# Window attention: tiles of 128 queries of one head become tiles of 64 queries of two heads, and a list scheduler orders the stage

## The chip, the cores and the metric

The kernel runs on one core of a Trainium2 chip. A core has five engines that work side by side, each through its own queue in order: TensorE (PE, matrix products and transpositions; its weight loads are PEld), VectorE (DVE), ScalarE (ACT), GpSimd (POOL) and SyncE (SP), which here issues most of the DMA transfers. PSUM is eight banks into which TensorE writes; SBUF holds the rest; both have 128 partitions. The metric is the device time of one execution in microseconds (us).

## The reference, cut to what matters

Three steps follow each other: attention with a causal window of 128 positions, a layer with a rational nonlinearity, a layer with an ELU.

```python
B, H, S, D = 4, 8, 576, 64
scores = q @ k.T / sqrt(D)                      # per batch entry and head
bias = -slopes[h] * abs(rel)                    # rel = query position - key position
mask = (rel >= 0) & (rel < 128)
attn = softmax(where(mask, scores + bias, -1e9))
x = (attn @ v), heads side by side              # (2304, 512)
h = x @ w_in;  x = (P(h) / Q(h)) @ w_out        # 512 -> 2048 -> 512, P and Q polynomials
h = x @ w_in2; out = elu(h) @ w_out2            # 512 -> 2048 -> 512
```

## The kernel before

All numbers are fp32 or fp32 split into a high and a low part for the large products. The attention runs in 16 units (`units`): a unit `u` is one batch entry and one pair of heads (`e` = 0, 1). Its steps have short names that the change keeps in spirit:

- `q_T`/`k_T` steps (`qT`, `kT`, `zT`) transpose q and k on TensorE; `qC`, `kC`, `zC` copy them out of PSUM to `qkT`. The last 64 positions (576 = 4 x 128 + 64) are a tail of their own, in the bank `ty`.
- `S0` to `S3` are the scores of 128 queries of each head against up to 256 keys (two products, one a head, on the two row halves of the array, each with a bank of its own); `S4` is the tail: 64 queries of both heads, stacked on the partitions, in one bank.
- `D0` to `D8` (`shifted`, VectorE) add the bias of the window and find the row's maximum in one instruction; `E0` to `E8` (`exp`, ScalarE) exponentiate and sum; `R0`, `R1` (`inverse`, VectorE) invert the sums; `N0` to `N8` (`normalise`, GpSimd) multiply.
- `T..` transpose the probabilities on TensorE, `C..` copy them out (ScalarE), `V0`, `V1`, `Y` multiply by v, `XC` and `XY` copy the unit's result into `xT`.

Beside it the stage converts the first layer's weights for the later products, key by key: `s` (ScalarE), `a`, `b`, `h`, `l` (`conv_scale`, `conv_shift`, `conv_or`, `conv_hi`, `conv_lo`), two keys a unit from the fourth unit on (`PLAN`), four more near the end (`CONV_AFTER`, where `conv_hi` is ScalarE's). Loads of q, k, v (`load`) and weights (`load_w`) are issued on SP.

What sets the order is the table `STEPS`: one period is run through step by step, and each step is for unit `t + late`, so that the units overlap. Towards the end the first four chunks of the next stage's first product (`early`, `AHEAD`) and the first two rational nonlinearities (`FIRST`) are put between. `experts` follows with the two layers.

## Time and profile before

| what | value |
|---|---|
| time, median of 3 runs | 932.98 us (931.71 to 934.49) |
| time of the profiled execution | 933.09 us |
| its span, first to last instruction | 931.4 us |
| busy in the span: TensorE, VectorE, ScalarE, GpSimd | 98%, 85%, 80%, 20% |
| granted TensorE clock | 0.998 of full |

The span is less than the execution's time by what lies ahead of the first and behind the last instruction. Busy shares are means over stages: the attention stage, about the first 150 us, is not limited as the rest is, where TensorE multiplies without a gap.

### The profile page before, as it was taken

To read this page: it belongs to the slowest core of one execution; us is meant where nothing else is said; L and a number is where in the kernel's file an instruction comes from. 1 tells how busy PE (TensorE), PEld (TensorE's weight loads), DVE (VectorE), ACT (ScalarE), POOL (GpSimd) and SP (SyncE) were. 2 spreads that over 40 slices of the span, in tenths; PEclk is the share of its full clock that TensorE was granted. 3 is DMA by queue.
4 is the path that set the end of the run, shared out by engine and by line. 5 is a ranking of instruction groups with operands and counts; after the bars stand their busy time and mean duration, and the time that the engine had idled before them with its cause. 6 is when DMAs were issued, how large, how long until landed. Compare 5 with 4: busy or idle time off the path is not lost.

```text
span 931.4 us, 16710 instructions
## 1 busy us (share of the span) xinstructions
PE 913.8 (98%) x5494; PEld 838.8 (90%) x5494; DVE 792.0 (85%) x1863; ACT 741.9 (80%) x1623; POOL 185.2 (20%) x260
## 2 busy tenths in 40 slices
PE   8999999999999999999999989999999999999998
PEld 5777778999999999999999988898989898888887
DVE  7899998998998998988989999998968688677653
ACT  6999999889898898889888987666876567767553
POOL 5566661122222222222222210000000000000000
PEclk9999999999999999999999999999999999999999
DMA  9899951012222212222200133445243323442201
GB/s 195 217 242 230 236 154 67 1 35 68 86 68 79 89 56 92 85 63 86 86 30 29 38 110 113 158 157 171 91 162 110 115 81 100 147 147 80 80 0 68
DMA packets 112423, 98.35 MB, mean 106 GB/s; under 512 B 62800, under 2 KB 86096, under 8 KB 112336
## 3 DMA queue, kind: packets, MB, share of 16 engines
q1 hardware_dynamic: 109936, 96.70, 35.2%
q10 hardware_dynamic: 2400, 0.59, 0.4%
q8 instruction: 43, 0.70, 0.3%
q14 instruction: 44, 0.36, 0.1%
HBM read 79.96 MB, written 17.30 MB: 104 GB/s over the span
## 4 chain that ended last, share of the span: by engine, by line
PE 79%; DVE 14%; ACT 3%; DMA 2%; issue 1%; DVEq 0%; ACTq 0%; SPq 0%
PE acc L923 21%; PE m L907 18%; PE acc L699 18%; PE h L251 18%; DVE pr_wi L494 2%; DVE pr_wo L494 1%; DVE cvt L146 1%; PE s_ps L468 1%; DVE qkT L437 1%; DVE ghi L292 1%; PE x L561 1%; DVE ee L313 1%; DMA q_wo<-in_q_dram 1%; PE ps_pT L542 1%; DVE w_wi L160 1%
## 5 line engine op out<-in xcount | busy, mean ns | idle before, releaser
L251 PE MATMUL h<-xs,w_wi 128*128 128x384 f32 x1152 | 216.9, 335 | 0.0
L251 PEld LDWEIGHTS h<-xs,w_wi 128*128 128x128 f32 x1152 | 200.7, 188 | 1.2 <-DVE xs L227 0.6
L699 PE MATMUL acc<-ghi,w_wo 128*128 128x384 f32 x768 | 194.8, 334 | 0.0
L310 POOL TENSOR_TENSOR glo<-ee,rr 128x384 fp32r<-128x384 f32 x92 | 93.7, 1018 | 312.4 <-DVE ee L309 109.3
L699 PEld LDWEIGHTS acc<-ghi,w_wo 128*128 128x128 f32 x768 | 138.6, 188 | 0.0
L699 PE MATMUL acc<-glo,w_wo 128*128 128x384 f32 x384 | 128.4, 334 | 0.5 <-DVE glo L310 0.5
L923 PE MATMUL acc<-op_wo,ghi 128*128 128x512 f32 x288 | 90.0, 393 | 0.0
L907 PE MATMUL m<-xo_wo,op_wi 128*128 128x384 f32 x336 | 77.0, 337 | 2.3 <-DVE ee L963 2.3
L907 PE MATMUL m<-xo_wi,op_wi 128*128 128x384 f32 x336 | 78.0, 340 | 0.0
L969 ACT ACTIVATE oo<-qq 128x384 f32<-128x384 f32 x24 | 12.6, 526 | 77.0 <-DVE qq L963 77.0
L699 PEld LDWEIGHTS acc<-glo,w_wo 128*128 128x128 f32 x384 | 72.1, 188 | 0.8 <-DVE glo L310 0.8
L298 ACT ACTIVATE rr<-qq,c_q 128x384 f32<-128x384 f32 x96 | 59.2, 617 | 16.5 <-DVE qq L295 15.7
L281 ACT ACTIVATE oo<-h,a_sb 128x384 f32<-128x384 f32 x96 | 68.0, 708 | 3.3 <-DVE h L312 3.2
L284 ACT ACTIVATE ee<-h,a_sb 128x384 f32<-128x384 f32 x96 | 67.7, 705 | 0.0
L907 PEld LDWEIGHTS m<-xo_wo,op_wi 128*128 128x128 f32 x336 | 61.3, 189 | 6.4 <-ACT oo L973 2.5
L295 DVE SCALAR_TENSOR_TENSOR qq<-h,b_abs,qa 128x384 f32<-128x384 f32 x92 | 56.1, 610 | 12.4 <-ACT qa L280 11.3
L292 DVE TENSOR_TENSOR ghi<-ee,rr 128x384 fp32r<-128x384 f32 x96 | 53.5, 558 | 12.2 <-ACT h L279 0.5
L313 DVE TENSOR_TENSOR ee<-ee,h 128x384 f32<-128x384 f32 x96 | 53.3, 555 | 10.4 <-DVE h L312 0.5
L923 PEld LDWEIGHTS acc<-op_wo,ghi 128*128 128x128 f32 x288 | 53.8, 189 | 9.0
L907 PEld LDWEIGHTS m<-xo_wi,op_wi 128*128 128x128 f32 x336 | 61.1, 189 | 0.0
L279 ACT ACTIVATE h<-h 128x384 f32<-128x384 f32 x96 | 46.3, 483 | 14.8 <-PE h L251 14.2
L963 DVE TENSOR_TENSOR ee<-ee,m 128x384 f32<-128x384 f32 x96 | 52.8, 551 | 5.8 <-PE m L907 5.5
(192 smaller groups left out, 2068.4 us busy)
## 6 DMA issues: line engine op xcount, KB each, us to landing
pair<-joined_wo SPq DMA_DIRECT2D x43, 256.0 KB, 2.6
raw_wo<-in_moe_w_out_dram SPq DMA_DIRECT2D x20, 512.0 KB, 4.7
raw_wi<-in_moe_w_in_dram SPq DMA_DIRECT2D x16, 512.0 KB, 4.3
half<-in_moe_w_in_dram SPq DMA_DIRECT2D x32, 256.0 KB, 2.7
two_wo<-joined_wi SPq DMA_DIRECT2D x32, 256.0 KB, 2.8
s<-sums SPq DMA_DIRECT2D x32, 256.0 KB, 2.9
half<-in_moe_w_out_dram SPq DMA_DIRECT2D x22, 256.0 KB, 2.8
v<-in_v_dram SPq DMA_DIRECT2D x32, 128.0 KB, 3.3
```

Source lines behind the costliest of these rows:

```text
L251: nc.tensor.matmul(h, lhsT=WT["wi", f][:, SEL[wp], kk * P:(kk + 1) * P], rhs=x[xp][kk], start=(kk == 0 and n == 0), stop=(kk == KD - 1 and ...
L281: nc.scalar.activation(out=oo, in_=h2, func=AF.Identity, scale=a_sb[:, 3:4], bias=a_sb[:, 1:2])
L284: nc.scalar.activation(out=ee, in_=h2, func=AF.Identity, scale=a_sb[:, 2:3], bias=a_sb[:, 0:1])
L292: nc.vector.tensor_tensor(out=hi, in0=ee0, in1=rr0, op=ALU.mult)
L295: nc.vector.scalar_tensor_tensor(out=qq, in0=h2, scalar=b_abs[:, 1:2], in1=qa, op0=ALU.mult, op1=ALU.add)
L298: nc.scalar.activation(out=rr, in_=qq, func=AF.Ln, bias=c_q)
L310: (nc.gpsimd if c > 4 else nc.vector).tensor_tensor(out=low, in0=ee0, in1=rr0, op=ALU.mult)
L313: nc.vector.tensor_tensor(out=ee, in0=ee, in1=h, op=ALU.add)
L699: nc.tensor.matmul(acc_t[d], lhsT=WT["wo", f][:, SEL[wp], d * P:(d + 1) * P], rhs=gt[SEL[xp]], start=(f == 0 and n == 0), stop=(f == KF - ...
L907: nc.tensor.matmul(out, lhsT=w[:, SEL[wp], c0:c0 + P], rhs=XO[q // NP2, nm, k][:, SEL[xp]], start=(k == 0 and n == 0), stop=(k == 1 and n ...
L923: nc.tensor.matmul(acc_t[T, t], lhsT=gt[SEL[xp]][:, t * P:(t + 1) * P], rhs=w[:, SEL[wp]], start=(first and n == 0), stop=(last and n == 2),)
L963: nc.vector.tensor_tensor(out=t, in0=R[q, x], in1=M[q, m], op=ALU.add)
```

## The change

Attention is cut anew. A tile is now 64 queries (`Q`) of both heads stacked on the 128 partitions, nine tiles (`t` = 0 to 8) a unit, against the 64, 128 or 192 keys (`W`) that the window reaches; tiles alternate which head is on top. So the scores of a tile are two products on 64 x 64 corners of the array, and each of the steps `D`, `E`, `N` works on up to 192 columns where it had up to 256. Transposed probabilities are `T0` to `T3` (four or three blocks); the product with v is in 64-column pieces, even tiles in the bank `evens`, odd ones in `odds`, which also takes the last transpositions of q and k (`zC` copies these out). `XE` and `XO` copy the result out; `XY` is gone. The biases are rebuilt for this layout, all four pairs' early.

The table `STEPS` goes. `attention_steps` lists every step of the stage, loads, conversions (28 keys, `conv_hi` always on VectorE), the four chunks of the first product (`g`) and two nonlinearities (`r`) among them, each with its engine, a cost and what it needs; `in_time` then walks through them as a list scheduler with ranks (`rank`: 7600 a unit plus an offset of the step, `OFF`) and hands them out in order of the times it finds. Three banks of the next stage's first product rotate in another order.

```diff
-STEPS = (
-    ("T00", -1), ("a0", 1), ("l1", -1), ("C01", -1), ("S0", 1), ("S1", 1), ("C00", -1),
...
-    ("XC", -1), ("T01", 0),
-)
...
-PLAN = (0, 0, 0) + (2,) * 12 + (0,) * 4
-CONV_AFTER = ((15, "E8"), (15, "R1"), (14, "V1"), (15, "T01"), (15, "T11"), (15, "V1"))
-AHEAD = {
...
+UNITS = 16
+EARLY = 24
+LAG = {"PE": 250, "DVE": 150, "ACT": 190, "POOL": 180, "SP": 2300}
+UT = 7600
+MODE = {"qT": 0, "kT": 0, "T": 0, "S": 1, "V": 2}
+STAY = 800
...
+OFF = {
+    "ldq": -37303, "ldk": -40037, "ldv": -7307, "qT": 49228, "qC": -19956, "kT": -37687, "kC":
...
+def attention_steps():
+    todo = {}
+
+    def step(key, engine, cost, *needs):
+        todo[key] = (engine, cost, needs)
...
+    for u in range(UNITS):
+        p = u // 4
+        for n, nm in enumerate("qk"):
+            step(("ld", nm, u), "SP", 1550, (nm + "T", u - 2))
+        step(("ld", "v", u), "SP", 1550, ("V", u - 2, 1))
+        step(("qT", u), "PE", 590, ("ld", "q", u), ("ident",), ("consts",), ("kC", u - 1), ("zC", u - 1))
+        step(("kT", u), "PE", 590, ("ld", "k", u), ("ident",), ("consts",), *([("qC", u)] if u else []))
+        gone = [("S", u - 2, h) for h in range(2)]
+        step(("qC", u), "ACT", 477, ("qT", u), *gone)
+        step(("kC", u), "DVE", 603, ("kT", u), *gone)
+        step(("zC", u), "DVE", 200, ("kT", u), ("qT", u), *gone)
+        for h in range(2):
+            n = 2 * u + h
+            gone = []
+            for a in (2 * n - 3, 2 * n - 2):
+                v, g = divmod(a // 2, 2)
+                ts = [(0, 2, 4), (6, 8), (1, 3), (5, 7)][2 * (a % 2) + g]
+                gone += [("D", v, t) for t in ts]
+            step(("S", u, h), "PE", 750 - 110 * h, ("qC", u), ("kC", u), ("zC", u),
+                 ("S", u - 1 + h, 1 - h), *gone)
+        for t in range(9):
+            m = max(t - 1, 0) // 2
+            c = cols(t)
+            step(("D", u, t), "DVE", {64: 140, 128: 207, 192: 277}[c], ("S", u, int(t > 4)), ("bias", p),
+                 ("T", u - 2, m))
+            step(("E", u, t), "ACT", {64: 331, 128: 385, 192: 440}[c], ("D", u, t))
+            step(("N", u, t), "POOL", {64: 330, 128: 400, 192: 480}[c], ("R", u, int(t > 4)), ("E", u, t))
+        step(("R", u, 0), "DVE", 320, *[("E", u, t) for t in range(5)])
+        step(("R", u, 1), "DVE", 320, *[("E", u, t) for t in range(5, 9)])
+        for m in range(4):
+            v, w = divmod(4 * u + m - 2, 4)
+            step(("T", u, m), "PE", 440 if m == 0 else 330, *[("N", u, t) for t in tiles(m)], ("C", v, w),
+                 ("T", u - (m == 0), (m - 1) % 4))
+            step(("C", u, m), "ACT", 477 if m == 0 else 370, ("T", u, m), ("V", u - 1, m // 2))
+        for h in range(2):
+            step(("V", u, h), "PE", 1000, ("C", u, 2 * h), ("C", u, 2 * h + 1), ("ld", "v", u), ("XE", u - 1),
+                 ("XO", u - 1), *([("V", u, 0)] if h else []))
+        step(("XE", u), "ACT", 317, ("V", u, 0), ("V", u, 1))
+        step(("XO", u), "ACT", 264, ("V", u, 0), ("V", u, 1))
...
+        step(("ldw", n), "SP", 1550, *gone, ("ldw", n - 1))
+        if n >= EARLY + 4:
+            continue
+        step(("cs", n), "ACT", 588, ("ldw", n), ("cl", n - 3), ("cs", n - 1))
+        step(("ca", n), "DVE", 337, ("ldw", n))
+        step(("cb", n), "DVE", 577, ("cs", n), ("ca", n))
+        step(("ch", n), "DVE", 310, ("cb", n))
+        step(("cl", n), "DVE", 603, ("ch", n))
...
+    while len(order) < len(todo):
+        best = None
+        for engine, cand in ready.items():
+            if cand:
+                at = max(min(cand.values()), free[engine])
+                if best is None or at < best[0]:
+                    best = at, engine
+        at, engine = best
+        ends = MODE.get(last)
+        key = min(
+            (k for k, t in ready[engine].items() if t <= at + 40),
+            key=lambda k: ranks[k] + (engine == "PE" and MODE.get(k[0], ends) != ends and STAY),
+        )
...
+        if engine == "PE":
+            cost += 100 * (MODE.get(key[0], ends) != ends)
+            last = key[0]
+        free[engine] = at + cost
+        done[key] = at + cost + LAG[engine]
+        order.append((at, len(order), key))
...
-    def early():
-
-        for c in range(4):
-            yield from gemm1(c, c, x1[0], 4 + c)
...
-            def scores_tail(u):
-                qk = qkT_t[u]
-                s_t[u, 0] = sp = s_bank([P, P + TL])
-                for e in range(2):
-                    r0 = e * D
-                    nc.tensor.matmul(
-                        sp[e * TL:(e + 1) * TL, :],
-                        lhsT=qk[r0:r0 + D, 0, NF * P:S],
-                        rhs=qk[r0:r0 + D, 1, (NF - 1) * P:S],
-                        start=True, stop=True,
-                    )
-
-            def scores(i):
...
-                    for e in range(2):
-                        if i % 2 == 0:
-                            t = s_bank([P, 2, 2 * P])
-                            s_t[u, 1 + 2 * i + e] = t[:, 0]
-                            s_t[u, 3 + 2 * i + e] = t[:, 1]
-                        r0 = e * D
-                        nc.tensor.matmul(
-                            s_t[u, 1 + 2 * i + e][:, c0:2 * P],
-                            lhsT=qk[r0:r0 + D, 0, i * P:(i + 1) * P],
-                            rhs=qk[r0:r0 + D, 1, k0:k0 + 2 * P - c0],
-                            start=True, stop=True,
+                    r = raw_t["qk"[n], u]
...
+            def scores(u, h):
+
+                in_even, in_odd = [bank(next(s_banks), [P, 4 * P], "s_ps") for _ in range(2)]
+                qk = qkT[u % 2]
+                for t in ((0, 2, 1, 4, 3), (6, 5, 8, 7))[h]:
+                    w = min((t + 1) * Q, W)
+                    n = 2 if t == 0 else (t - 1) // 2 % 2
+                    s_t[u, t] = (in_odd if t % 2 else in_even)[:, n * W:n * W + w]
+                    for e in range(2):
+                        at = (e + t) % 2 * Q
+                        r = slice(e * D, (e + 1) * D)
+                        nc.tensor.matmul(
+                            s_t[u, t][at:at + Q], lhsT=qk[r, 0, t * Q:(t + 1) * Q],
+                            rhs=qk[r, 1, (t + 1) * Q - w:(t + 1) * Q], start=True, stop=True,
+                        )
...
+            def shifted(u, t):
+                sp = s_t.pop((u, t))
+                nc.vector.tensor_tensor_reduce(
+                    out=probs(u, t), in0=sp, in1=bias[units[u][1]][t % 2][:, W - sp.shape[1]:W],
+                    scale=-SC, scalar=BIG, op0=ALU.add, op1=ALU.min, accum_out=stat(u, 0, t, t + 1),
+                )
...
+            def attn_v(u, h):
+
+
+                vr = raw_t["v", u]
+                if h == 0:
+                    x_t[u] = bank(3, [P, NF + 1, Q], "evens")
+                todo = []
+                for m in (2 * h, 2 * h + 1):
+                    pT = pT_t[u, m]
+                    for e in range(2):
+                        todo.append((0, 0, e, m + 1, vr[:, m, e], pT[:, 2 + e]))
+                        todo.append((0, 1, e, m, vr[:, m, e], pT[:, 1 - e]))
+                        todo.append((1, 0, e, m + 1, vr[0:Q, m + 1, e], pT[0:Q, 4 + e]))
...
+                    nc.tensor.matmul(
+                        (x_t[u], odds)[to][e * D:(e + 1) * D, n], lhsT=lhsT, rhs=rhs,
+                        start=(to, e) not in begun, stop=(to, e) not in left,
                     )
...
+            def x_copy(n):
                 def run(u):
                     b, p = units[u]
-                    copy(eng, xT[:, p, b * S + NF * P:(b + 1) * S], ty[:, 2, :])
+                    x = xT[:, p, b * S:(b + 1) * S].rearrange("r (t c) -> r t c", c=Q)
...
-                for step, late in STEPS:
-                    run(step, t + late)
-                    if t < NU - 1 or not 0 <= t + late < NU:
...
-                    if (t + late, step) in CONV_AFTER:
-                        conv_step(to_conv, to_conv[0] not in LATE[4:])
-                    if (t + late, step) == FIRST["r0"]:
-                        rational(0)
...
+            for _, _, (name, *args) in in_time(attention_steps()):
+                if name != "ld" or args[0] == "v" or args[1] > 1:
+                    RUN[name](*args)
```

Three places of the order. The first is TensorE's queue in the middle of the stage; `s_ps` are scores, `ps_pT` transposed probabilities, `ps_qk` transposed q or k, `x`, `ty`, `evens`, `odds` products with v. Before:

```order
L542 MATMUL ps_pT<-ident,pr_wi_104 128x128 x3
L542 MATMUL ps_pT<-ident,rr_99 128x128
L542 MATMUL ps_pT<-ident,pr_wi_104 128x128 x4
L468 MATMUL s_ps<-qkT_101 128x128 x2
L468 MATMUL s_ps<-qkT_101 128x256 x2
L542 MATMUL ps_pT<-ident,pr_wo_105 128x128 x4
L412 MATMUL ps_qk<-ident,k_wo_1239 128x128 x4
L542 MATMUL ps_pT<-ident,pr_wo_105 128x128 x3
L542 MATMUL ps_pT<-ident,rr_99 128x128
L450 MATMUL s_ps<-qkT_101 64x192 x2
L468 MATMUL s_ps<-qkT_101 128x256 x4
```

After, a stretch of the same length in the stage:

```order
L581 MATMUL ps_qk<-ident,q_wo_89 128x128 x4
L581 MATMUL odds<-ident,q_wo_89 128x128
L675 MATMUL odds<-pT,v_93 64x64 x2
L675 MATMUL evens<-pT,v_93 64x64 x2
L675 MATMUL odds<-pT,v_93 64x64 x2
L675 MATMUL evens<-pT,v_93 64x64 x4
L675 MATMUL odds<-pT,v_93 64x64 x2
L675 MATMUL evens<-pT,v_93 64x64 x4
L645 MATMUL ps_pT<-ident,pr_wo_104 128x128 x3
L608 MATMUL s_ps<-qkT_99 64x192 x8
L645 MATMUL ps_pT<-ident,pr_wo_104 128x128 x3
```

Scores of 128 queries against 256 keys have become eight products of 64 x 192 in a row, and the product with v is 16 products of 64 columns at a time where it was 14 of 128 and 4 of 64 in three groups.

The second place is the copy of the last q and k columns of unit 15 from `odds`. On TensorE, after the transpositions of k into `odds`, the order now is:

```order
L581 MATMUL ps_qk<-ident,k_wo_91 128x128 x4
L581 MATMUL odds<-ident,k_wo_91 128x128
L645 MATMUL ps_pT<-ident,pr_wi_101 128x128 x3
L675 MATMUL odds<-pT,v_93 64x64 x2
L675 MATMUL evens<-pT,v_93 64x64 x2
L675 MATMUL odds<-pT,v_93 64x64 x2
L675 MATMUL evens<-pT,v_93 64x64 x2
L675 MATMUL odds<-pT,v_93 64x64 x2
L675 MATMUL evens<-pT,v_93 64x64 x2
L675 MATMUL odds<-pT,v_93 64x64 x2
L675 MATMUL evens<-pT,v_93 64x64 x2
```

and on VectorE the copy and its neighbours:

```order
L311 TENSOR_TENSOR w_wo_2153<-cvt_2123,w_wo_2153 128x512
L559 COPY qkT_99<-ps_qk 128x512
L629 TENSOR_SCALAR qq_100<-qq_100 128x5
L630 RECIPROCAL qq_100<-qq_100 128x5
L287 TENSOR_SCALAR raw_wi_2121<-raw_wi_2121 128x512
L559 COPY qkT_99<-odds 128x2x64
L615 ISA pr_wi_101,qq_100<-s_ps,rr_97 128x128
```

The copy from `odds` stands in program order behind the product with v of unit 11 that also writes that bank; before, it read the bank `ty`, with the tails.

The third place is VectorE's queue at the end of the stage, up to the first low part `glo` that the next stage's second product takes. Before:

```order
L160 TENSOR_TENSOR w_wi_2374<-cvt_2311,w_wi_2374 128x512
L295 SCALAR_TENSOR_TENSOR qq_2385<-h_2383,b_abs,qq_2385 128x384
L312 TENSOR_TENSOR h<-oo,h 128x384
L313 TENSOR_TENSOR ee_2384<-ee_2384,h 128x384
L160 TENSOR_TENSOR w_wo_2412<-cvt_2350,w_wo_2412 128x512
L437 COPY xT<-ty 128x64
L292 TENSOR_TENSOR ghi_2458<-ee_2328,rr_2331 128x384
L304 SCALAR_TENSOR_TENSOR qq_2329<-qq_2329,ghi_2458 128x384
L309 TENSOR_TENSOR ee_2328<-ee_2328,qq_2329 128x384
L310 TENSOR_TENSOR glo_2459<-ee_2328,rr_2331 128x384
```

After:

```order
L428 TENSOR_TENSOR h<-oo,h 128x384
L429 TENSOR_TENSOR ee_2606<-ee_2606,h 128x384
L305 CAST w_wi_2668<-cvt_2639 128x512
L287 TENSOR_SCALAR raw_wo_2614<-raw_wo_2614 128x512
L311 TENSOR_TENSOR w_wi_2668<-cvt_2639,w_wi_2668 128x512
L297 SCALAR_TENSOR_TENSOR cvt_2673<-cvt_2673,raw_wo_2614 128x512
L305 CAST w_wo_2697<-cvt_2673 128x512
L311 TENSOR_TENSOR w_wo_2697<-cvt_2673,w_wo_2697 128x512
L458 TENSOR_TENSOR ghi_2715<-ee_2520,rr_2523 128x384
L470 SCALAR_TENSOR_TENSOR qq_2521<-qq_2521,ghi_2715 128x384
L475 TENSOR_TENSOR ee_2520<-ee_2520,qq_2521 128x384
L476 TENSOR_TENSOR glo_2716<-ee_2520,rr_2523 128x384
```

The last conversions (L305 casts the high part, L311 subtracts it) and the second nonlinearity stand there as before; the casts of the high part are new in VectorE's queue, and the copies of the result from `ty` are gone.

## Rows read from the trace of the kernel before

**Rows 1.** The page of the profile: its first line.

```profile
span 931.4 us, 16710 instructions
```

**Rows 2.** Busy time by stretch, with its sum (stretch, length, engine busy and count).

```profile
core 0: us, PE busy (x) PEld busy (x) DVE busy (x) ACT busy (x) POOL busy (x), PEclk, DMA share, GB/s
0.00:9.20 9.20, 7.23 (x28) 3.43 (x28) 2.85 (x7) 2.48 (x3) 5.63 (x24) 1.00 1.01 171
...
60.00:120.00 60.00, 58.33 (x584) 43.21 (x584) 59.52 (x237) 59.30 (x187) 39.97 (x66) 1.00 0.94 226
...
sum 155.00, PE 143.86 PEld 107.74 DVE 138.71 ACT 143.34 POOL 91.51; mean PE 23.98 PEld 17.96 DVE 23.12 ACT 23.89 POOL 15.25
```

**Rows 3.** Timeline of TensorE (start, length, line, tiles, count): scores of two units.

```profile
60.58 0.93 PE L468 MATMUL s_ps<-qkT 64*128 64x128 f32 x8
...
77.55 0.71 PE L468 MATMUL s_ps<-qkT 64*128 64x128 f32 x6
```

**Rows 4.** Timeline of TensorE at the handover.

```profile
155.19 0.44 PE L699 MATMUL acc<-glo,w_wo 128*128 128x384 f32 x1 [0.51 <-DVE glo L310]
...
157.05 2.24 PE L251 MATMUL h<-xs,w_wi 128*128 128x384 f32 x12
```

**Rows 5.** Timeline of ScalarE: copies, exponentials, rounding of x.

```profile
76.83 0.58 ACT L435 ACTIVATE xT<-x 128x512 f32<-128x512 f32 x1
77.31 1.06 ACT L435 ACTIVATE pT<-ps_pT 128x512 f32<-128x512 f32 x2
...
81.80 0.51 ACT L509 ACTIVATE pr_wo<-pr_wo,qq 128x256 f32<-128x256 f32 x1
...
83.36 0.46 ACT L509 ACTIVATE rr<-rr,qq 128x192 f32<-128x192 f32 x1
...
134.37 1.75 ACT L226 ACTIVATE xs<-xT 128x384 fp32r<-128x384 f32 x4
```

**Rows 6.** Timeline of VectorE: end copy, shift-and-reduce, cast.

```profile
77.76 0.22 DVE L437 COPY xT<-ty 128x64 f32<-128x64 f32 x1
...
80.57 0.28 DVE L494 CUSTOM_DVE_ANT_0 pr_wo<-s_ps,oo 128x128 f32<-128x128 f32 x1
...
81.99 0.35 DVE L494 CUSTOM_DVE_ANT_0 rr<-s_ps,bias_t 128x192 f32<-128x192 f32 x1
...
82.87 0.41 DVE L494 CUSTOM_DVE_ANT_0 pr_wi<-s_ps,h 128x256 f32<-128x256 f32 x1
...
126.61 0.39 DVE L154 CAST w_wo<-cvt 128x512 fp32r<-128x512 f32 x1
```

**Rows 7.** Timeline of VectorE before its first shift-and-reduce.

```profile
4.37 0.34 DVE L389 SCALAR_TENSOR_TENSOR bias_t<-relmask_wi 64x192 f32<-64x192 f32 x1
...
9.21 0.29 DVE L494 CUSTOM_DVE_ANT_0 pr_wi<-s_ps,bias_wo 128x128 f32<-128x128 f32 x1 [1.38 <-PE s_ps L468]
```

**Rows 8.** Timeline of TensorE, unit 13 and its neighbours.

```profile
124.51 1.75 PE L561 MATMUL x<-pT,v 128*64 128x128 f32 x28
126.09 0.40 PE L572 MATMUL ty<-pT,v 128*64 128x64 f32 x8
...
127.44 0.93 PE L468 MATMUL s_ps<-qkT 64*128 64x128 f32 x8
128.30 0.98 PE L542 MATMUL ps_pT<-ident,pr_wo 128*128 128x128 f32 x7
```

**Rows 9.** Groups of TensorE by shape, 60 to 120 us: count | busy us, mean ns | idle.

```profile
L542 PE MATMUL ps_pT<-ident,pr_wi 128*128 128x128 f32 x54 | 8.5, 280 | 0.0
...
L450 PE MATMUL s_ps<-qkT 64*64 64x192 f32 x28 | 3.8, 348 | 0.0
```

**Rows 10.** Chain that ended last (start, length, what).

```profile
43.35 6.34 DMA q_wo<-in_q_dram
```

**Rows 11.** DMA from 60 to 120 us.

```profile
DMA packets 29959, 13.57 MB, mean 226 GB/s; under 512 B 25578, under 2 KB 29054, under 8 KB 29950
```

More of the change, by code (lines that the diff above doesn't have):

```diff
@@ new lines, in in_time @@
+def in_time(todo):
+    users = {}
+    for key, (_, _, needs) in todo.items():
+        for n in needs:
+            if n in todo:
+                users.setdefault(n, []).append(key)
+    ranks = {key: rank(key) for key in todo}
+    missing = {key: sum(n in todo for n in set(needs)) for key, (_, _, needs) in todo.items()}
+    ready = {e: {} for e in LAG}
+    for key in todo:
+        if not missing[key]:
+            ready[todo[key][0]][key] = 0
+    free, done, order, last = dict.fromkeys(LAG, 0), {}, [], None
+    while len(order) < len(todo):
[11 more added lines that the diff above has]
+        )
+        at = max(at, ready[engine].pop(key))
+        cost = todo[key][1]
+        if engine == "PE":
[4 more added lines that the diff above has]
+        order.append((at, len(order), key))
+        for u in users.get(key, []):
+            missing[u] -= 1
+            if not missing[u]:
+                ready[todo[u][0]][u] = max(done[n] for n in set(todo[u][2]) if n in todo)
+    return sorted(order)
@@ L362, in rel_and_mask @@
+            work = place(order[22], [P, 4, W], F32, "relmask")
+            base, mask, base_t, mask_t = [work[:, n] for n in range(4)]
+            even = xs.tile([P, NP, W], F32, tag="x2", name="bias_even")
+            odd = [row(t, cols=2 * W) for t in ("ee1", "rr1")]
+            bias = [(even[:, p], odd[p // 2][:, p % 2 * W:(p % 2 + 1) * W]) for p in range(NP)]
             def rel_and_mask(rel, msk, first):
@@ L396, in attention @@
-            qkT_t, s_t, p_t, pT_t, pT_ps, stat, tp_ps, x_t = {}, {}, {}, {}, {}, {}, {}, {}
-            pt = [row(f"rr{n}", cols=2 * P) for n in range(2)]
+                for half in range(2):
+                    rel, msk = ((base, mask), (base_t, mask_t))[half]
+                    rows = slice(half * Q, (half + 1) * Q)
+                    for o in range(2):
+                        slope = 2.0 ** (-8.0 * (2 * p + (half + o) % 2 + 1) / H)
+                        nc.vector.scalar_tensor_tensor(
+                            out=bias[p][o][rows], in0=rel[rows], scalar=slope / SC, in1=msk[rows],
+                            op0=ALU.mult, op1=ALU.add,
+                        )
@@ L418, in qk_copy @@
[L418 to L431 removed]
+            s_t, pT_t, pT_ps, tp_ps, x_t = {}, {}, {}, {}, {}
@@ new lines, in attention, with probs_T, probs_T_copy @@
+            p_banks = cycle((0, 1))
+            def probs_T(u, m):
+                n = 3 + (m == 0)
+                pT_ps[u, m] = ps = bank(next(p_banks), [P, n, P], "ps_pT")
+                pr = pair(u, m)
+                for slot, block in enumerate((2, 0, 1)):
+                    nc.tensor.transpose(ps[:, slot], pr[:, block * P:(block + 1) * P], ident)
+                if m == 0:
+                    nc.tensor.transpose(ps[:, 3], prob[u % 2][0][:, 0:P], ident)
+            def probs_T_copy(u, m):
+                ps = pT_ps.pop((u, m))
+                pT_t[u, m] = t = ptp.tile([P, 2 * ps.shape[1], Q], F32, tag=f"pT{m}", name="pT")
+                copy("ACT", t.rearrange("p k c -> p (k c)"), ps.rearrange("p s c -> p (s c)"))
@@ L684, in attention @@
-            run_all(ahead)
+            t = bank(3, [P, 4 * P], "warm")
+            for _ in range(2):
+                nc.tensor.matmul(t, lhsT=zero[:, 0:P], rhs=zero, start=True, stop=True)
+            for key in [("ld", nm, u) for u in range(2) for nm in "kq"]:
+                load(*key[1:])
+                if key == ("ld", "q", 0):
+                    nc.scalar.preload_act_table_set("natural_log_exp_and_others")
+            for _, _, (name, *args) in in_time(attention_steps()):
+                if name != "ld" or args[0] == "v" or args[1] > 1:
+                    RUN[name](*args)
```

447 lines of the change are left out of this document (191 added, 256 removed), and 17 rows, old and new, of tables (OFF, STEPS).

## The prediction

> **What bounds the kernel now.** I read the page's span first [rows 1]: the profiled execution took 933.09 us, 1.7 us of it around the span of 931.4 us, and lies 0.1 us above the median of the three timed runs (932.98). The sum below is made against 933.1. A difference of 0.3%, 2.8 us, is what a measurement of this kernel can tell from no change.
>
> Next the table of stretches [rows 2]. The change edits the attention stage and the handover to the matrix stage alone, so the question is which engine paces that stage. From 60 to 120 us VectorE is busy for 59.52 and ScalarE for 59.30 of 60 us: both are full, neither hides the other. TensorE shows 58.33, but its ends are modelled and pipelined, so it needs an estimate of its own (below). The granted clock is 1.00, that is 2.4 GHz, throughout, so no clock term enters.
>
> Then the timeline of TensorE, to find the length of a unit (one pair of heads of one batch entry): the scores of one unit begin at 60.58, those of the second after it at 77.55 us [rows 3], so a unit takes 8.48 us. Sixteen such units make the stage. Behind it TensorE runs matrix multiplications without a gap: its fifth chunk of the first product begins at 157.05 us [rows 4], and from there on both programs hold the same work. What the attention stage saves until that point is what the kernel saves.
>
> **The change part by part.**
>
> *ScalarE, exponentials.* A unit has nine exponentials before and after. Before they are 6 of 256, 2 of 128 and 1 of 192 columns, 1984 in all; after, 64 + 128 + 7 x 192 = 1536. Lengths of 0.46 and 0.51 us for 192 and 256 columns [rows 5] give 0.05 us for 64 columns. The 448 columns fewer are 7 steps: 0.35 us a unit.
>
> *ScalarE, copies.* Four copies of 512 columns become one of 512 and three of 384, and the copy of the unit's result (512) becomes two of 320 and 256. One copy of 512 is 0.58 us long and two are 1.06 [rows 5], so each holds the engine for 0.48. For 384 columns the nearest row, four in 1.75 us [rows 5], gives (1.75 - 0.1) / 4 = 0.41 each, from SBUF and not from PSUM; the exponentials' slope gives 0.38. By the first the copies lose 0.02 us a unit (the extra instruction eats it), by the second they save 0.20. I take 0.15, nearer the slope, since source and engine stay the same there. ScalarE's unit is then 0.50 us shorter (0.33 to 0.55): 8.0 us over 16 units. Four casts of weights that ScalarE did in the last units go to VectorE, which frees about 2 us more: 10 us in all (7.4 to 11).
>
> *VectorE.* The nine shift-and-reduce instructions lose the same 448 columns. 128, 192 and 256 columns are 0.28, 0.35 and 0.41 us long [rows 6], 0.07 for 64 columns: 0.49 us a unit. The copy of the unit's last 64 results, 0.22 long of which the next instruction overlaps part, is gone: 0.13 (nothing to 0.22). That is 0.62 us a unit, 9.9 us in 16. The biases stay 16 instructions, eight of them shorter by some 0.07: 0.6 saved. The four casts come back as at most 4 x 0.39 us [rows 6]: 1.5 lost. Together 9.0 us (7 to 10.5).
>
> *Head.* Three pairs' biases now stand ahead of the first shift-and-reduce, which before began at 9.21 us; at 0.34 us each [rows 7] that start slips by 2.5 us. It costs nothing in the sum: the twelve instructions stood among later units before, in VectorE's full time, and here fill idle time or time already counted.
>
> *TensorE.* Matrix products in fp32 are two instructions each; two that use different halves of the array run side by side. The 28 instructions of 128 columns from 124.51 to 126.09 us [rows 8] are 14 pairs at 0.113 us, 0.88 ns a column. A change of array shape shows as what is left of the rows behind it: 0.33 us for 4 pairs of 64 columns, and 0.86 for 768 columns of scores, leave 0.1 to 0.2; I take 0.15. A transposition is (0.98 - 0.16) / 7 = 0.117. Before, a unit is: scores 1.58 and 0.34, product with v 1.58 and 0.22, 26 transpositions 2.9, some 8.5 changes 1.3; together 7.9 of 8.48 us. After: 23 transpositions 2.7, product with v 32 pairs of 64 columns 1.8, changes 9 x 0.15 = 1.35, and the scores, 18 products on 64 x 64 corners of the array. If the four corners run at once, the larger diagonal has 2 x (448 + 384) columns: 1.46 us, sum 7.3. If only two do, 3072 columns take 2.70, sum 8.55. No row shows four at once. The nearest is the tail's scores on two corners (two heads, one bank, different partitions): 28 instructions of 348 ns are 9.7 us of work, yet busy for 3.8, 2.6 at a time; the same ratio for transpositions on the full array, whose ends overlap alone, is 54 x 280 ns to 8.5 us, 1.8 [rows 9]. So two corners overlap. I take four.
>
> With four, TensorE's 7.3 fits below VectorE's 8.48 - 0.62 = 7.86 us and ScalarE's 7.98, and these two set the unit.
>
> *The rule that speaks against it.* The Trainium skill, "TensorEngine Tiling (Array Packing)", section on restrictions and gotchas, says that different row tiles cannot access the same PSUM bank simultaneously. Both heads of a tile here write one bank from different row halves. By that rule at most two corners would overlap and the scores would take 2.70 us by the price above, the unit 8.55; the row of the tail's scores, two row halves into one bank and 2.6 at a time, speaks against it.
>
> *New waits.* VectorE's copy of the last q and k columns reads the bank `odds`, which now also takes half of each product with v. Five of the sixteen copies stand in program order behind such a product, as in the order shown of unit 15, and wait for it with all of VectorE behind them: at most 0.9 us each (half of 1.8), 4.5 in all, nothing where the product is done. I take 0.
>
> *Loads.* A unit brings 0.88 MB of q, k, v (3 x 2 x 576 x 64 numbers of 4 bytes) and two loads of weights of 512 KB; at 7.9 us that is 245 GB/s, against a mean of 226 from 60 to 120 us, and the chain that ended last passes through a load of q for 6.3 us in one early unit [rows 10, 11]. Weights are issued far ahead and cover this; I take 0, and up to 3 us lost if they don't.
>
> *Tail.* Before, the second product's first low part arrives at 155.19 us [rows 4], at the end of VectorE's queue. After, VectorE still ends with conversions and the two nonlinear chunks, as the order shows; TensorE has only the last quarter of one chunk behind the last product with v, where before it had two chunks. Either way VectorE's total decides, counted above.
>
> Sum: both engines shed 9 to 10 us; the lesser, VectorE's 9.0, counts: 933.1 - 9.0 = 924.1.
>
> **The rivals.**
> - *Both engines shed their columns and stay full* (forecast): 924, with the bounds of the costs 920.5 to 927.5.
> - *The new order leaves waits.* For it: three engines at over 90% of the unit in fixed queues, new waits on `odds` (up to 4.5 us) and loads at 245 GB/s (up to 3 us). Against: VectorE's and ScalarE's waits from 60 to 120 us come to under 1 us each today [rows 2], in an equally tight order. The gain falls to 2 to 5 us: 928 to 931.
> - *The four corners don't overlap* (other side). Place: the scores on TensorE, a unit of 8.55 us or more plus the waits that TensorE has today (8.48 - 7.9, at least a part): 16 x (0.07 to 0.25) = 1 to 4 us lost, 934 to 937. It decides from 2.6 us of scores a unit.
> - *The scheduler also fills idle time.* VectorE is busy for 138.71 of the first 155 us and for 2.85 of the first 9.2 [rows 2]; 9.9 us of idle time lie between. If half goes, 5 us more: 919.
> - *The change doesn't do what it says*: the columns are fewer in the program itself, so the work is saved in any case; only where it goes is open.
>
> **How the numbers follow.** Forecast 0.57, waits 0.20, corners 0.10, filled idle time 0.11, loads or something unseen that slow it 0.02. Time 924, range 919 to 931: it holds the forecast, the waits and half of the filled idle time, and leaves out the corners (0.10) and the far half of the filled time (0.06). The forecast's own range is 920.5 to 927.5. Faster by over 0.3% (below 930.2): 0.57 + 0.11 + 0.13 of the waits = 0.81. Within 0.3%: 0.07 of the waits, 0.04 of the corners = 0.11. Slower: 0.06 of the corners and 0.02 = 0.08.
>
> **What would show it.** In the timeline, scores of successive units some 7.9 us apart and the fifth chunk of the first product near 148 us; the exponentials' sum a unit down by 0.35; scores of four instructions starting within 20 ns of each other and a group of ten products done in 0.75 us (1.4 us would be two corners). Waits of the copy from `odds` for a product with v, and VectorE idle for more than 10 us between its first shift and 146 us, would show the second rival; gaps of TensorE ended by loads of q or k the part of the loads. The prediction is wrong if VectorE and ScalarE are no longer the full engines from 60 to 110 us, or if the stage behind 157 us differs in length.

## The result, and the profile after

| kernel | median of the runs | lowest to highest | ratio to before, 95% interval |
|---|---|---|---|
| before | 932.37 us | 931.71 to 934.49 | |
| changed | 938.36 us | 937.85 to 939.59 | 1.0062 (1.0042 to 1.0082) |

The change makes the kernel 6 us slower; 924.0 was forecast. The page's first line [rows 1]:

```profile
span 936.1 us, 18028 instructions
```

The table of stretches of the changed kernel, for [rows 2]: two rows of the head, one of the middle of the stage, two of the handover, and, from a second view, the sum over the first 155 us.

```profile
core 0: us, PE busy (x) PEld busy (x) DVE busy (x) ACT busy (x) POOL busy (x), PEclk, DMA share, GB/s
10.00:15.00 5.00, 2.34 (x17) 1.48 (x17) 4.90 (x26) 2.88 (x12) 0.00 (x0) 0.81 0.81 207
15.00:20.00 5.00, 4.52 (x34) 3.80 (x34) 4.07 (x21) 4.37 (x17) 3.48 (x8) 0.51 0.71 139
60.00:120.00 60.00, 55.41 (x944) 42.14 (x936) 53.08 (x229) 56.57 (x200) 36.56 (x68) 0.99 0.90 218
150.00:155.00 5.00, 1.72 (x5) 0.89 (x5) 4.83 (x11) 1.19 (x4) 0.00 (x0) 0.80 0.01 2
155.00:160.00 5.00, 4.48 (x14) 4.48 (x15) 4.72 (x10) 4.97 (x10) 0.00 (x0) 0.51 0.00 0
...
sum 155.00, PE 133.48 PEld 100.56 DVE 129.84 ACT 132.84 POOL 85.06; mean PE 33.37 PEld 25.14 DVE 32.46 ACT 33.21 POOL 21.26
```

The work is gone as forecast: in the first 155 us VectorE is busy for 129.84 us, 8.9 less than in [rows 2] (9.0 forecast), and ScalarE for 132.84, 10.5 less (10). But neither engine is full any more: from 60 to 120 us they have 6.9 and 3.4 us idle, where they had 0.5 and 0.7. Idle time took the place of the work. (At 155 us both programs stand at the same step, the first low part on VectorE, so the two sums hold nearly the same work.)

The timeline of TensorE tells where: scores of the third and the sixteenth unit, then the handover [rows 3, 4].

```profile
22.00 0.98 PE L608 MATMUL s_ps<-qkT 64*64 64x64 f32 x20
...
125.27 0.98 PE L608 MATMUL s_ps<-qkT 64*64 64x64 f32 x20
...
153.74 1.01 PE L769 MATMUL acc<-ghi,w_wo 128*128 128x384 f32 x2 [3.03 <-DVE ghi L458]
155.52 0.69 PE L769 MATMUL acc<-glo,w_wo 128*128 128x384 f32 x1 [0.77 <-DVE glo L476]
...
158.88 1.31 PE L402 MATMUL h<-xs,w_wi 128*128 128x384 f32 x4
```

In the kernel before, the same marks stand at 18.81, 127.44 [rows 8] and, for the fifth chunk, 157.05 us [rows 4]; the first of them is this row.

```profile
18.81 0.93 PE L468 MATMUL s_ps<-qkT 64*128 64x128 f32 x8
```

| mark | before | forecast (0.62 a unit; 9.0 at the end) | changed | lost against the forecast since the mark above |
|---|---|---|---|---|
| scores of unit 3 | 18.8 | 17.6 | 22.0 | 4.4 (head) |
| scores of unit 16 | 127.4 | 118.1 | 125.3 | 2.7 (middle) |
| fifth chunk | 157.05 | 148 | 158.9 | 3.7 (tail) |
| span | 931.4 | 922.4 | 936.1 | 2.9 (behind the stage) |

Together 13.7 us. The mean unit between the first two marks is (125.27 - 22.00) / 13 = 7.94 us. That is near the 7.86 forecast, but over the same units the kernel before takes (127.44 - 18.81) / 13 = 8.36, not the 8.48 of the two units that the prediction read; so a unit gained 0.42 us of the 0.62 forecast. Still, 11 of the 13.7 us lie at the two ends and behind the stage.

The waits of VectorE from 20 to 145 us (us in total, times, longest): for weights in transfer 3.9 us, for the bank of the product with v 1.9, for the scaled weight of ScalarE 2.5. The last row is of the kernel before, where the same copy waited for the bank `ty`.

```profile
DVE cvt L297 <- ACT cvt L279: 2.5, 6, 0.6
DVE raw_wo L287 <- DMA raw_wo<-in_moe_w_out_dram: 2.1, 2, 1.5
DVE raw_wi L287 <- DMA raw_wi<-in_moe_w_in_dram: 1.8, 2, 1.2
...
DVE qkT L559 <- PE evens L675: 1.1, 1, 1.1
...
DVE qkT L559 <- PE odds L675: 0.8, 2, 0.7
```

```profile
DVE qkT L437 <- PE ty L572: 1.2, 1, 1.2
```

### The profile page after: what moved, and what is told of

The parts are those of the page before. It is cut to its first block, busy times and chain, and to the rows that moved or that the text cites. A ratio compares the mean times of both kernels' runs of the same rounds, so it can differ in the third digit from the quotient of the medians.

```text
span 936.1 us, 18028 instructions
## 1 busy us (share of the span) xinstructions
PE 906.1 (97%) x6148; PEld 834.2 (89%) x6148; DVE 783.4 (84%) x1851; ACT 731.6 (78%) x1635; POOL 178.7 (19%) x264
## 4 chain that ended last, share of the span: by engine, by line
PE 76%; DVE 5%; ACT 2%; issue 1%; POOL 0%; DVEq 0%; ACTq 0%
PE acc L993 21%; PE acc L769 19%; PE m L977 19%; PE h L402 18%; DVE ghi L458 1%; DVE ee L479 1%; DVE qq L461 1%; DVE ee L475 1%; DVE qq L470 1%; DVE h L478 0%; ACT rr L464 0%; ACT rr L465 0%; DVE xo_wo L934 0%; DVE xo_wi L934 0%; DVE t_wi L955 0%
## 5 line engine op out<-in xcount | busy, mean ns | idle before, releaser
L769 PE MATMUL acc<-ghi,w_wo 128*128 128x384 f32 x768 | 197.3, 338 | 3.0 <-DVE ghi L458 3.0
L479 DVE TENSOR_TENSOR ee<-ee,h 128x384 f32<-128x384 f32 x94 | 52.2, 555 | 10.2 <-DVE h L478 0.5
```

The costliest lines, as they stand in the source:

```text
L479: nc.vector.tensor_tensor(out=ee, in0=ee, in1=h, op=ALU.add)
L769: nc.tensor.matmul(acc_t[d], lhsT=WT["wo", f][:, SEL[wp], d * P:(d + 1) * P], rhs=gt[SEL[xp]], start=(f == 0 and n == 0), stop=(f == KF - ...
```

## The experiments

Each timed run stands against the kernel before on the same chip. The changed kernel was run once more beside them.

> The changed kernel once more, beside the others of this group, since single runs of its relatives lay up to 7 us apart. Theory: it stays at 938 with runs within 2 us of each other. Rival: its waits follow the arrival of loads and it spreads as they do, over 936 to 942.

938.14 us (936.78 to 939.37), ratio 1.0054 (1.0040 to 1.0068). It stays. Its relatives with fewer waits spread more: see the last section.

**Behind the stage: the banks.** The last line of the diff turns the rotation of the first layer's banks. The list of the first banks that the second layer's products write (`m_first`) was not turned with it.

```diff
@@ e1_bank, in the changed kernel @@
-        m_first = [7, 4, 6, 7, 4, 6, 7]
+        m_first = [5, 7, 6, 5, 7, 6, 7]
@@ e6_before_bank, in the kernel before @@
-        m_first = [7, 4, 6, 7, 4, 6, 7]
+        m_first = [4, 5, 6, 4, 5, 6, 7]
```

> The changed kernel, but the first products of the second layer write the banks that come free first (5, 7, 6 in place of 7, 4, 6). Theory: the change turned the rotation of the first layer's banks to 7, 4, 5 and left that list as it was, so the first two products wait for the last two chunks' banks (1.3 and 2.9 us of TensorE idle at 542 and 545 us); with the list turned too, the gap of TensorE at that place falls to about 0.3 us and the time by 2.4 us, to 936.0. Rival: VectorE's chain sets that boundary whatever bank is written; the wait goes to a later product and less than 0.5 us is gained (938).

> The kernel before with the one change that its second layer's first products write the banks 4, 5, 6 in place of 7, 4, 6, so each waits for one chunk later, as in the changed kernel. Theory: it loses what the changed kernel lost at that place, 2.4 to 2.7 us: 935.2. Rival: VectorE's chain sets the boundary and the list of banks does not matter: 932.5.

935.11 us (1.0028, 1.0016 to 1.0040), and 935.93 us (1.0031, 1.0019 to 1.0044). One list takes some 3 us off the changed kernel and puts 3 us on the kernel before. TensorE's waits from 515 to 565 us in the kernel before, in the changed one, and in the kernel before with the list spoiled (three views, one after the other):

```profile
PE m L907 <- DVE ee L963: 2.3, 1, 2.3
PE m L907 <- DVE ee L313: 0.2, 1, 0.2
```

```profile
PE m L977 <- DVE ee L479: 4.2, 2, 2.9
```

```profile
PE m L907 <- DVE ee L313: 4.1, 2, 2.9
```

The products wait for VectorE's last read of the bank (L479, L313), twice, and the longest wait is the same 2.9 us in both programs. The waits alone differ by only 1.7 us (4.2 against 2.5). The rest, as an estimate, is the clock: behind the longer wait it falls from 545 us on, behind the wait of 2.3 us in the kernel before it falls less, from 555 us on (the changed kernel, then the one before).

```profile
545.00:550.00 5.00, 2.26 (x7) 2.26 (x8) 4.26 (x9) 4.03 (x9) 1.27 (x2) 0.56 0.01 3
```

```profile
555.00:560.00 5.00, 3.52 (x13) 3.55 (x14) 3.95 (x9) 4.62 (x11) 0.00 (x0) 0.73 0.22 61
```

**The head.** In the changed kernel the shift-and-reduce starts at 11.42 us behind the biases of three pairs, and TensorE waits for it, ahead of this row of its timeline:

```profile
12.57 0.76 PE L608 MATMUL s_ps<-qkT 64*64 64x192 f32 x10 [2.58 <-DVE qq L615]
```

```diff
@@ e2_bias @@
+LATER = {("bias", p): ("D", 2 * p - 1, 7) for p in range(1, 4)}
+    at = {key: t for t, _, key in steps}
+    return sorted((at[LATER[key]] + 1 if key in LATER else t, n, key) for t, n, key in steps)
@@ e17_warm, behind the step ("qT", 1) @@
+                    for _ in range(3):
+                        nc.tensor.matmul(t, lhsT=zero[:, 0:P], rhs=zero, start=True, stop=True)
```

> The changed kernel, but the biases of pairs 1 to 3 are computed behind units 1, 3 and 5 and not ahead of the first shift-and-reduce. Theory: the late first shift (11.4 us, 9.2 before) is what holds TensorE for 2.6 us at 10 us and is carried through to the end of the stage; the first shift comes at about 9.0 us, the gap and the lower clock of 10 to 20 us go, the fifth chunk comes 2 us earlier, 936.3. Rival: later waits (for weights, banks, the tail's queue) take up what the head gives; scores of unit 3 come 2 us earlier, those of unit 15 do not, 938.

> The changed kernel in its own order, with three products of 512 columns on zeros put into TensorE's gap of 2.6 us at 10 us. Theory: the lower clock of 10 to 20 us follows from that gap; it stays at 1.00 and the scores of the third unit begin about 1 us earlier (22.0 us in the changed kernel), the time falls by 0.5 to 1 us. Rival: the products themselves hold the scores back, or the clock falls all the same: no gain, 938.

The biases moved: 937.50 us, but from 933.64 to 941.43, so the median tells it from 938.14 no more than the interval does (1.0037 to 1.0078). Its profile is of the run of 933.64. There the scores of unit 3 come at 18.41 us, 3.6 earlier, those of unit 16 at 122.00 and the handover at 155.59, both 3.3 earlier, with the tail's gap of 3.03 us as it was. This is the fastest of seven runs, and where the slower ones lose it again no profile shows. In it the clock is 1.00 from 9.2 to 20 us:

```profile
9.20:20.00 10.80, 8.70 (x117) 6.03 (x115) 8.92 (x50) 10.13 (x39) 5.36 (x11) 1.00 0.90 198
```

The warming products: 937.66 us (1.0037 to 1.0073), no gain to be told. But the clock stays at 1.00 through the head and the scores of unit 3 begin at 21.05 us, 0.95 earlier, with the biases where they were. Of the 3.6 us about 1 is the clock's, which fell behind the gap, and the rest the biases'.

```profile
15.00:20.00 5.00, 3.62 (x50) 2.60 (x50) 4.89 (x24) 4.97 (x21) 3.63 (x8) 1.00 0.67 147
```

**The loads.**

```diff
@@ e4_loads @@
+    return sorted((t - 8000 if key[0] == "ldw" and 0 < key[1] < 22 else t, n, key) for t, n, key in steps)
@@ e10_noload, in load(nm, u); e11_before_noload likewise @@
+                if u > 1:
+                    return
```

> The changed kernel, but each of the weight loads 1 to 21 is issued some 8 us earlier in the queue of loads. Theory: VectorE's four waits of 0.6 to 1.5 us for a weight (at 39, 54, 100 and 105 us, 4 us together) come from loads that are issued about 4 us ahead of their use; issued a unit earlier they are gone and the time falls by 2 to 4 us, 934.5 to 936.5. Rival: the queue of loads is as full as the engines; the waits move to q, k and v, which now stand behind the weights: 938, or slower.

> The changed kernel without the loads of q, k and v from the third unit on: all later units use the data of the first two, so the output is not the reference's; every other step stays. Theory: the order itself leaves the waits, through queues in which each step stands behind one that waits for another engine; without these loads the weight loads come early too, the waits for loads go (4 us and what hangs on them), and the time falls by 3 to 5 us, 933 to 935, with VectorE and ScalarE still idle for more than 6 us each from 20 to 145 us. Rival: the loads pace the stage, since they share 90% of its transfer time; without them it runs at what the engines need, 7.9 us a unit, and the time falls by 8 us or more, 930 or less.

> The kernel before without the loads of q, k and v from the third unit on, as in the run beside it (output not the reference's). Theory: VectorE and ScalarE were full at 8.48 us a unit, loads cost it only the early waits of some 2 us: 930.5 to 932.5. Rival: the loads set its 8.48 us a unit as well; the time falls by 5 us or more.

Weight loads issued earlier: 938.71 us (1.0039 to 1.0073), nothing gained. In its profile, of a run of 935.10, VectorE's waits for weights are gone, but it waits 3.8 us for scores, where the changed kernel waits 2.4, and longer for `odds` and sums: part of the wait moved, and in the median all of it. Without the loads of q, k and v: 934.52 us (1.0019, 1.0010 to 1.0028), 3.6 less than the changed kernel; the kernel before gains 1.6 (0.9984, 0.9975 to 0.9993). So loads cost the changed kernel about 2 us more than the one before, inside the bound of 3 that the prediction gave and did not take. They don't pace the stage: with transfers at little over a third of their share (0.32 for 0.85), the 125 us from 20 to 145 us still hold 14.8 us of idle VectorE. But part of the middle is theirs: ScalarE is idle for 4.2 us, where more than 6 were expected, and the mean unit between the two marks is 7.62 us for 7.94.

```profile
20.00:145.00 125.00, 115.22 (x1892) 89.75 (x1891) 110.21 (x460) 120.79 (x414) 75.60 (x138) 0.98 0.32 107
```

**The tail.** Two rows of VectorE's timeline in the changed kernel: the 27th key's second step on VectorE waits 3.2 us for ScalarE, and the first high part stands behind the conversions of two keys. It comes at 153.14 us, no earlier than in the kernel before (the third row), for all the work that is gone. TensorE, with one quarter of a chunk left, waits 3.03 us for it (above), and its clock falls to 0.51: 14 products from 155 to 160 us [x14 in the table above], where e3_tail, below, does 31 at full clock.

```profile
148.40 0.69 DVE L297 SCALAR_TENSOR_TENSOR cvt<-cvt,raw_wi 128x512 int32<-128x512 int32 x1 [3.17 <-ACT cvt L279]
...
153.14 0.55 DVE L458 TENSOR_TENSOR ghi<-ee,rr 128x384 fp32r<-128x384 f32 x1
```

```profile
152.82 0.55 DVE L292 TENSOR_TENSOR ghi<-ee,rr 128x384 fp32r<-128x384 f32 x1
```

```diff
@@ e3_tail @@
-        if n >= EARLY + 4:
+        if n >= EARLY + 2:
             continue
```

> The changed kernel with 26 in place of 28 weight conversions in the attention stage; the last two are done in the matrix stage, one by one, as the other four. Theory: the first high part stands in VectorE's queue behind these two, and TensorE's gap of 3.0 us at 150.7 us and the clock of 0.51 behind it follow from that; the gap falls below 1 us, the clock stays at 1.00, the fifth chunk comes at 154 to 155.5 us instead of 158.9: 934 to 935. Rival: the gap is held by the end of the last product with v, or the conversions are missed in the matrix stage: 938 or more.

943.01 us (1.0090 to 1.0120), slower, and yet the first half is nearly as expected: the gap is 1.16 us (below 1 was expected), the clock stays at 1.00, the fifth chunk comes at 155.30, and the same products as at 176 us in the changed kernel come 4.0 us earlier. Then the rival's second half comes: the 15th chunk finds its weights unconverted, TensorE waits 5.8 us, and behind that the clock is 0.54 from 205 to 210 us.

```profile
PE h L402 <- ACT w_wi L307: 4.4, 1, 4.4
PE h L402 <- DVE w_wi L311: 1.4, 1, 1.4
PE acc L769 <- DVE glo L476: 1.2, 1, 1.2
```

**The four corners.**

```diff
@@ e5_corners @@
-                        at = (e + t) % 2 * Q
+                        at = e * Q
```

> The changed kernel, but both heads keep their place in every tile, so that only two of the array's four corners are used by the scores (odd tiles then get the other head's bias and the wrong half of v: the output is not the reference's). Theory: four corners run at once in the changed kernel (its ten products of the first half take 0.9 us from start to the next group); with two, a group takes 1.4 us or more, TensorE's unit grows by 1.0 to 1.2 us, and the time by 5 to 15 us. Rival: products into one bank from different rows of the array do not run at once anyway, a group takes as long as before, 938.

947.45 us (1.0143, 1.0122 to 1.0163), 9.3 more. The same twenty instructions, in the profile of the changed kernel [rows 3] 0.98 us long (above), take here:

```profile
73.99 1.53 PE L608 MATMUL s_ps<-qkT 64*64 64x64 f32 x20
```

From a group's start to the next group's, undisturbed, it is 0.87 to 1.03 us against 1.41 to 1.46. So four corners do run at once, as the prediction took it, though a group takes more than its 0.75 us. The mean unit grows to 8.42 us, by 0.5 and not by the 1.0 to 1.2 expected.

**The edits together.** e12_three is e1_bank, e2_bias and e3_tail with two more conversions at the start of the matrix stage, so that no chunk finds its weights missing; e9_four has e4_loads too.

```diff
-            if j == 0 and f % 2 and f > 2:
+            if j == 0 and f > 2 and (f % 2 or f in (4, 6)):
```

> The changed kernel with four of its waits taken away together: the second layer's banks, biases 1 to 3 later, weight loads a unit earlier, and 26 conversions ahead of the matrix stage with two conversions more at its start, so that none is missed there. Theory: the waits are separate and add up, 2.7 + 2.3 + 2.2 + 4 us: 927, faster than both kernels, the fifth chunk at 151 to 153 us. Rival: they hide one another or the odds bank and the tail's chain hold the stage: 931 to 934.

> The changed kernel with three of the four edits together: the second layer's banks, biases 1 to 3 later, 26 conversions ahead of the matrix stage with two more at its start; the weight loads stay where they are. Theory: the loads moved up took time from q and k (TensorE idle for 2.1 us at 14.8 and 2.3 us at 81.3 us); without that the three gains show: 929 to 931. Rival: the spread of the loads' arrival decides and the order of the queue does not: 932 to 933, as with all four.

932.70 us (1.0001, 0.9989 to 1.0013) and 931.61 us (0.9989, 0.9975 to 1.0003): back at the kernel before, not beyond it. The gains don't add up as expected, and earlier weights add nothing: with them TensorE waits 2.6 us for q, without them 1.8. The profile of e12_three tells which gain is lost. Its scores of unit 3 come at 18.75 us, 3.25 earlier than in the changed kernel, but those of unit 16 at 125.42, no earlier: a unit now takes 8.2 us, and the order gives back in the middle what the head gained, as the rival of e2_bias had it. What stays is the tail's gain, the fifth chunk at 154.35 us and so 4.5 earlier, and that of the banks.

**The order.** Same steps, edits of e12_three but for the place of the biases, and a written order in place of `in_time`. It was searched for by moving one step at a time within what it needs, and keeping what shortened a replay of the queues with the durations of these traces: 1.25 us for a pair's biases (0.8 in the change's table), 4.5 us and more from issue to landing of a load (3.85), the waits on the bank `odds` (none). The four parts of a nonlinearity are also called by number; in the change a part can run in the place of another, when the scheduler takes the fourth step ahead of the third.

```diff
@@ e13_order @@
-            for _, _, (name, *args) in in_time(attention_steps()):
+            for name, *args in in_order():
+ORDER = """
+ldk.0 ldq.0 ldk.1 ldq.1 ldw0 consts ldv.1 ident kT0 kC0 ldk.2 rel rel_t bias0 bias1 qT0 qC0 zC0 S0.0 ldq.2
+bias2 D0.1 D0.4 E0.4 qT1 D0.0 D0.2 S0.1 D0.6 ldw1 E0.0 E0.2 qC1 D0.3 E0.1 E0.3 D0.7 E0.7 D0.8 kT1 zC1 kC1
...
```

> The same tiles of 64 and the same steps as the run with three edits, but all of them in another order, one searched for with the durations that the traces show (biases 1.25 us, loads 4.5 us and more from issue to landing, one wait per bank for the copies from odds). Theory: the tiles save what was forecast, and the order loses it; an order made with the measured durations brings the fifth chunk to 146 to 152 us and the time to 922 to 928, faster than both kernels. Rival: four resources at 90% leave waits in any order once arrivals vary: 930 to 936.

924.53 us (923.95 to 924.77), ratio 0.9912 (0.9899 to 0.9925): 8.3 us faster than the kernel before. Its span, the scores of units 3 and 16, and the handover:

```profile
span 922.7 us, 18059 instructions
```

```profile
21.58 0.98 PE L510 MATMUL s_ps<-qkT 64*64 64x64 f32 x20 [0.22 <-DVE qkT L461]
...
115.96 0.98 PE L510 MATMUL s_ps<-qkT 64*64 64x64 f32 x20
...
144.11 0.44 PE L671 MATMUL acc<-glo,w_wo 128*128 128x384 f32 x1 [1.16 <-DVE glo L378]
...
145.98 2.24 PE L298 MATMUL h<-xs,w_wi 128*128 128x384 f32 x12
```

The head is better than the changed kernel's by 0.4 us only, and its clock falls too (0.71 from 10 to 15 us, 0.60 from 15 to 20), but the mean unit is (115.96 - 21.58) / 13 = 7.26 us and the fifth chunk comes at 145.98. Busy time from 20 to 145 us before, after the change, and in this order (three views):

```profile
20.00:145.00 125.00, 119.17 (x1202) 90.79 (x1200) 118.13 (x467) 122.93 (x382) 80.11 (x134) 1.00 0.85 212
```

```profile
20.00:145.00 125.00, 112.43 (x1845) 86.38 (x1844) 110.50 (x458) 118.24 (x406) 76.35 (x137) 0.99 0.85 217
```

```profile
20.00:145.00 125.00, 115.81 (x1926) 91.08 (x1926) 118.05 (x472) 122.20 (x422) 77.04 (x137) 1.00 0.86 218
```

VectorE and ScalarE idle for 6.9 and 2.1 us before, 14.5 and 6.8 in the changed order, 7.0 and 2.8 in the new one: as full as before, with less work in each unit. Not all of the 11.1 us that the fifth chunk comes earlier than in the kernel before are saved: two conversions, some 3 us of VectorE's work, are moved behind the stage (VectorE is busy for 130.25 us up to that mark, 133.54 in the changed kernel), and from the mark to the end the kernel takes 776.7 us, 2.4 more than the one before.

**The work given back.** Is it the columns, then, or the order alone?

```diff
@@ e14_both; e15_dve has the second, e16_act the first alone @@
+                if t == 8:
+                    nc.scalar.activation(out=pads[0], in_=pads[0], func=AF.Exp, scale=-1.0)
+                if t == 8:
+                    nc.vector.tensor_tensor(out=pads[1], in0=pads[1], in1=pads[1], op=ALU.subtract)
```

> The reordered kernel with about the work given back that tiles of 64 save: once a unit ScalarE computes one exponential of 384 columns more (0.5 us) and VectorE one subtraction of 384 columns more (0.5 us), on data that nothing uses. Theory: the columns saved are what makes the reordered kernel fast; both engines stay as full as they are, the stage grows by 16 x 0.4 to 0.5 us, 930.5 to 932.5, back at the kernel before. Rival: the order alone makes it fast and idle time takes the work up: below 927.5.

> The reordered kernel with VectorE's subtraction alone given back (0.5 us a unit). Theory: VectorE and ScalarE are both near the length of the unit, so either alone costs a part: 926 to 930. Rival: VectorE has 2 us in 60 us to spare and takes it up: 924.5 to 926.

> The reordered kernel with ScalarE's exponential alone given back (0.5 us a unit). Theory: ScalarE is busy for 59.4 of 60 us there and sets the unit: 929.5 to 932.5. Rival: TensorE or the queues set it: below 927.

932.13 us (0.9995, 0.9984 to 1.0005) with both, 930.62 (0.9979, 0.9968 to 0.9990) with VectorE's, 928.29 (0.9956, 0.9943 to 0.9968) with ScalarE's. Given back, the saved work costs 7.6 us and the kernel is where it was before. So this order has no room to hide that work, and without the saving it is no faster than the kernel before. Either engine alone costs a part, VectorE's 6.1 us, somewhat above what was expected, ScalarE's 3.8; that ScalarE alone sets the unit was wrong.

## Why the prediction was wrong, by its own steps

- *ScalarE and VectorE, exponentials, copies, shifts*: right in mechanism and size (8.9 and 10.5 us less busy).
- *The step that failed*: "these two set the unit" and "both engines ... the lesser, VectorE's 9.0, counts". A sum of saved work became time as if both queues stayed full. In the changed order they do not: from 20 to 145 us they idle for 14.5 and 6.8 us, where it was 6.9 and 2.1. In another order of nearly the same steps they do, and the time is 924.5. That this meets the forecast of 924 so closely is partly chance: the stage is 2 us shorter than forecast, with work moved out of it, and what follows is 2.4 us longer.
- *Head, "costs nothing in the sum"*: wrong. The slip of 2.5 us was rightly sized (2.2: the first shift at 11.42, from 9.21 [rows 7]); but it left TensorE idle for 2.58 us, the clock fell behind it, and unit 3 came 3.2 us late. "No clock term enters" fell with it: the rows of the stage read 1.00 before, and the change made the gap.
- *New waits on `odds`, 0*: 1.9 us measured, within its bound of 4.5; the copy's wait on `ty` before was 1.2, so 0.7 is new and 0 was nearly right. *Loads, 0*: some 2 us net, within its bound of 3. "Weights are issued far ahead and cover this" was wrong: VectorE waits 3.9 us for them.
- *Tail, "VectorE's total decides"*: wrong. Its total was lower by what was forecast, yet the first high part came no earlier (153.14 us, from 152.82): VectorE waited 3.2 us for a scaled weight with conversions ahead of the first high part; the two chunks that covered such a wait before were, as the prediction had seen, a quarter of one now. Gap and clock took 3.7 us. That the gap follows from the conversions is shown by e3_tail.
- *"From there on both programs hold the same work"*: the same work, but not the same banks: some 3 us of waits and of the clock behind them, shown from both sides by e1_bank and e6_before_bank. The prediction had the line in its diff and did not ask which bank comes free first where the rotation ends. Nor does TensorE multiply "without a gap" there: in the kernel before it waits 2.5 us at this place, and its clock is 0.73 from 555 to 560 us.
- *TensorE, four corners at once*: right, 0.9 us a group (priced at 0.75) and 1.4 with two. *The rule that speaks against it*: the Trainium skill, "TensorEngine Tiling (Array Packing)", section on restrictions and gotchas, has it that row tiles do not access one PSUM bank at the same time. Both heads of a tile write one bank from different row halves, and four corners take two thirds of the time that two take; the measurement decides, and as a limit on the time the rule does not show here.
- *The rival "the new order leaves waits"* was the mechanism, at a chance of 0.20 and priced at 928 to 931. It counted the waits that the prediction could name and not those that an order made with wrong durations leaves everywhere, at the two ends above all.
- Two small slips in its sums change no forecast: by the exponentials' slope the copies save 0.17 us and not 0.20, and 26 transpositions at 0.117 are 3.0 us and not 2.9.

Whether the kernel before would gain from a new order too, or from two conversions less in its stage, was not tried. That it has little to give is argued and not shown: from 20 to 145 us its idle time, 6.9 and 2.1 us, is what the new order has left too. How much the parts of the nonlinearities in each other's place cost alone was not tried either.

## What to carry to other kernels

Work taken off two full engines becomes time only if the order keeps them full: price the order by its idle time, as well as the steps, and give a scheduler durations and landing times from a trace. Where a change turns a rotation of buffers, follow it to its end and see which buffer the next stage takes first. Giving saved work back tells whether the new order would have had room for it.

## What the runs showed of the hardware

TensorE's clock fell to half, 1.2 GHz (granted 0.51 in a row of 5 us), behind gaps of 2.6 and 3.0 us in this single core's stage, and stayed at full where the 2.6 us were filled with products on zeros. Behind the gap at 150.7 us this halved the rate of a stage that TensorE paces, so a wait of 3 us cost more than 3 us. Such falls are not the changed kernel's alone: at the boundary to the second layer the kernel before reads 0.73 behind a wait of 2.3 us, the changed one 0.56 behind waits of 1.3 and 2.9 us.

Some of the kernels spread from run to run: e12_three took 928.67 us at a mean granted clock of 1.000 and 935.82 at 0.993, e2_bias 933.64 at 0.996 and 941.43 at 0.983. The longer runs are those with the lower clock; what sets off the gaps in some runs (the arrival of loads is a guess) was not settled. In the new order four runs lay within 0.8 us.
